# The written order of the opening dealt anew: linear attention followed by four expert layers on one core

## The chip, the cores and the metric

The kernel runs on one core of one Trainium2 chip. A core has five queues that each run their own list of instructions in order: PE (matmuls, with its weight loads PEld), ACT, DVE, POOL and SP. SP only issues DMAs; ACT and POOL issue some too. The metric is the device time of one launch in microseconds. Three runs of the kernel before gave 486.61 us as the median (486.33 to 486.74).

## What is computed

```python
def phi(x):                      # elu + 1
    return np.where(x > 0, x, np.exp(x) - 1.0) + 1.0
q_p, k_p = phi(q), phi(k)        # q, k, v: (8, 8, 576, 64), float32
kv = np.einsum('bhsd,bhse->bhde', k_p, v)
z  = np.sum(k_p, axis=2)
attn = einsum(q_p, kv) / (einsum(q_p, z)[..., None] + 1e-06)
x = attn.transpose(0, 2, 1, 3).reshape(4608, 512)
p = domain_probs / (domain_probs.sum(-1, keepdims=True) + 1e-09)
for e in range(4):               # w1: (4, 512, 1024), w2: (4, 1024, 512)
    out += p[:, e:e+1] * (np.maximum(x @ w1[e], 0) @ w2[e])
```

## The kernel before

**Tiles.** A batch has 576 rows: 512 make a tile, and the last 64 of each of the eight batches make a ninth tile. Tile j needs the attention of batch j, so the attention of batch j+1 is computed between the expert products of tile j. Each tile then passes four experts (two layers each); an expert is worked on as a unit (j, e) in two halves d.

**Layer 1** of a unit is a product of 2x2 blocks made with seven products instead of eight: steps p1, p2, p6, p7, p5, p4, p3 and the add c22 (class Block, L890 to L926). They need sums of weight blocks, made once by DVE: s{e}.0 to s{e}.3 (`weight_sums`, L745 to L751) for the first weights and t{e}.0 to t{e}.3 (L762 to L768) for the second, and sums of x blocks, ts{j}.0 to .3 (`token_sum`, L849). PE's products stand in L868 (`products`), ACT's copies in L879 and L894, the relu's in L901 and L922, and DVE's add with relu in L852. In the opening, tile 0 with expert 0 has a plain layer 1: steps L{g}{hf} (`layer1_half`, L655 and L664).

**Layer 2** of tile 0 is plain: y{e}.{ns}{part} (`layer2_part`, L715). From tile 1 on it is again made of seven products, m{j}{e}.{p}{i} (L810), that need sums of hidden blocks on POOL, hs{j}{e}.{d}{i} (L777 to L783). Results are weighted and added into `acc`, by ACT for the first (L704) and by DVE for the rest (L706), and stored by SP (L687). A step of several parts is written once for each part: for m10.51 the first mention emits its matmuls, the second its eviction.

**The opening.** Attention of batch 0 has its own code (class First): loads lq0-3, lk0-3, lv0-3 (L540, L548), exp on ACT (ke, qe: L563, L581), the linear part and the minimum on DVE or POOL (kl, ql, km, qm: L566, L584, L570, L587), the cast of v (vc: L573), transposes of q (qT: L595, copied in L597), kv products (kv: L606, copied in L617), numerators and denominators (nd: L628, divided in L631 and L632) and transposes of x (xT: L642, copied in L644). warm0 to warm4 are 14, 3, 2, 1 and 5 matmuls on zeros whose result nobody reads (L997).

**Loads of weights and of batch 1** are issued by POOL: w{layer}{e}{r} is a chunk of the first or second weights of expert e (L224, L227, L230); k0-3, v0-3, q0-3 are parts of batch 1 (L319); rk, rv its last 64 rows (L297). At most eight DMAs of POOL, and eight of SP and ACT together, are in flight: an issue waits for the landing of the one eight before. Later batches are loaded by SP: b1.load0 to 5 are the first six of batch 2's twelve loads, b2.load0 to 5 the other six, b1.loadlq the last 64 rows of batch 1's q, b1.next those of batch 2. The raw parts of all batches share six buffers (`praw`).

**The order** is explicit: each engine runs its instructions as they were emitted. CFG["EARLY"] (L87 to L119) is one list of step names; `advance` runs the next part of each named step, and each part puts its instructions at the end of the lists of the queues that it uses. EARLY covers the opening, tile 0 and half of tile 1; after it the steps left follow by numbers (the loop at the end). A queue runs its list strictly in order, so an instruction that waits holds all that stand behind it on its queue.

Of the kernel before, what the change touches and what calls it, by code (L numbers as in the profile page):

```python
# [84 lines left out]
    "WARM": (14, 3, 2, 1, 5),  # L85
    "BANK": {'qT0': 'py', 'qT1': 'b', 'nd00': 'py', 'nd00+': 'b', 'kv2': 'py', 'xT00': 'b', 'kv3': 'b', 'nd10+': 'b', 'L00': 'b', 'L10': 'py', 'nd01': 'b', 'xT01': 'py', 'nd11+': 'b', 'L20': 'e', 'L30': 'e', 'L01': 'e', 'L11': 'py', 'L21': 'py', 'L31': 'b', 'b1.qT3': 'py', 'b1.nd30': 'py', 'b1.nd21': 'b', 'b1.q1': 'b', 'b1.qT1': 'py', 'b1.nd01': 'py', 'b1.xT2': 'b', 'b1.nd11': 'py', 'b1.xT0': 'b'},
    "EARLY": (  # L87
        "lq2 lq3 lq0 lk0 qe0 ql0 ql3 qm0 kl0 lk1 lpr0 ke0 km0 qe2 ql2 qm2 lv0 ke1 kl1 km1 warm0 qT0 lv1 lk2 qe3 qm3 warm1 qT2 qT0 vc0 w100 warm2 kv0 vc1 qT2",
        "warm3 kv1 lk3 kv0 kv0 kl2 kv1 kl3 w102 kv1 nd01 lv3 nd01 warm4 xT11 xT01 ke2 km2 qT3 w103 vc3 lv2 ke3 vc2 nd00 w101 km3 xT01 w110 xT11 w111 kv3 k3 kv2",
        "qT3 lq1 nd00 qe1 xT00 w200 kv3 rk1 ql1 kv3 kv2 w201 qm1 L01 kv2 nd11 xT10 L31 qT1 v0 nd11 rv0 xT00 xT10 L10 xT21 rk0 xT21 v1 xT31 L11 qT1 xT31 nd10",  # L90
        "L01 L01 rv1 L31 w120 nd10 ts0.2 L00 ts0.0 xT30 ts0.1 xT20 L31 s0.0 L20 xT20 L30 xT30 L10 L10 L00 L00 L30 ts0.3 L30 p1.011 s1.0 p1.010 L11 L20 p1.010",
        "p2.010 s1.1 L20 w121 p2.010 p1.011 L21 L21 L21 s1.2 p6.010 p5.010 w210 L11 s1.3 p6.011 y0.30 p2.011 p6.010 p7.010 w211 p7.010 s0.1 p6.011 c22.010 v2",
        "y0.31 y0.00 p4.010 p2.011 y0.32 y0.33 p5.011 b1.k3 k0 pr0 y0.33 t0.0 t0.1 b1.km3 p7.011 p7.011 c22.011 y0.01 y0.02 y0.03 p4.010 b1.lk y0.20 y0.03 k2",
        "p4.011 s0.2 p3.010 p4.011 p3.011 y0.21 y0.10 y0.22 p3.010 y0.11 b1.v0 q1 k1 p1.021 y0.23 p1.021 p3.011 p1.020 s2.0 y0.12 v3 p2.021 b1.lv p1.020 t0.3",
        "s2.1 p2.020 s2.3 s2.2 y0.23 b1.v1 q0 t0.2 p6.020 p6.020 y0.13 p6.021 y0.13 y1.20 p7.020 y1.21 p2.020 p5.020 p7.020 w130 p2.021 y1.22 y1.23 t1.0 y1.10",
        "w131 p5.021 b1.v2 q3 b1.lkm y1.11 p6.021 b1.k0 b1.k2 b1.k1 w220 t1.1 t1.2 p7.021 y1.12 p7.021 c22.020 p3.020 y1.23 b1.v3 b1.km0 p4.020 p4.020 y1.00",
        "y1.01 q2 w221 y1.13 p4.021 b1.km2 b1.km1 b1.kv c22.021 p3.021 y1.02 y1.03 p1.030 p4.021 b1.q1 y1.30 y1.13 b1.load1 p1.031 b1.q0 p3.020 y1.31 p3.021",
        "p1.030 b1.qm1 b1.qT1 y1.32 y1.03 b1.qm0 s3.0 p1.031 w231 b1.qT0 s3.1 p2.030 y1.33 p6.030 b1.kv b1.qT0 p6.031 p2.031 b1.nd00 b1.nd01 b1.q3 p6.030 s3.3",
        "y1.33 p7.030 b1.loadlq p2.030 p5.030 b1.qm3 b1.qT3 p6.031 p7.030 w230 b1.qT1 b1.nd01 p7.031 p4.030 b1.qT3 s3.2 c22.030 b1.nd10 b1.nd11 b1.nd00 p2.031",
        "p3.030 b1.nd11 b1.nd10 p7.031 y2.00 y2.01 b1.nd30 p5.031 p4.031 p4.030 b1.next b1.nd31 b1.nd30 y2.20 b1.load0 b1.xT0 b1.lq b1.lqm b1.nd31 b1.q2 b1.qm2",  # L100
        "y2.21 b1.xT3 y2.02 c22.031 p4.031 b2.load2 y2.03 s0.3 b1.xT3 b1.qT2 y2.22 y2.23 b2.load1 b1.xT1 b1.load4 b1.load3 b1.load2 b1.qT2 b1.nd20 p3.031",
        "b1.xT1 p3.030 b1.nd21 y2.03 b1.xT0 b1.nd20 b1.nd21 y2.23 y2.10 y2.11 ts1.0 p1.101 p1.101 b1.load5 t1.3 b2.load0 t2.0 b1.xT2 y2.12 y2.13 b1.xT2 b2.k1",
        "ts1.1 lpr y2.30 y2.31 p1.100 p1.100 y2.32 y2.33 p3.031 p2.101 y3.20 y2.13 b2.km1 p6.100 b2.lk p2.100 t3.0 b2.load4 p2.101 p6.101 p6.100 p2.100 b2.lv",
        "ts1.2 p7.100 ts1.3 p7.100 b2.k0 y3.21 p5.100 y2.33 y3.22 t2.1 p4.100 y3.23 p6.101 p5.101 p4.100 p7.101 y3.30 c22.100 p3.100 b2.ones b1.qTl b2.v3 y3.00",
        "y3.01 p7.101 p4.101 b2.k2 b2.lkm y3.23 b2.km0 b2.load3 c22.101 b2.v1 y3.31 p3.100 t2.3 y3.32 p4.101 hs10.00 p3.101 b2.load5 y3.02 p1.110 b2.km2 y3.33",
        "p3.101 y3.03 b2.k3 b2.v0 b2.km3 b2.v2 b2.kv p1.110 y3.33 b2.load10 m10.21 b2.load7 p1.111 y3.03 y3.10 hs10.01 b1.qTl b2.q0 y3.11 p6.110 hs10.10",
        "hs10.02 y3.33 pr1 y3.12 y3.03 p1.111 m10.21 b2.q3 b2.load11 b2.qm0 y3.13 m10.51 hs10.11 p2.110 p6.111 p6.110 b2.q2 p2.111 m10.51 b2.qm3 y3.13 p2.110",
        "p6.111 t2.2 p7.110 m10.11 p5.110 m10.20 p7.110 b2.qm2 m10.11 b2.q1 c22.110 hs10.03 hs10.12 p7.111 m10.61 b2.qm1 t3.1 m10.20 p4.110 p4.110 p3.110",
        "p3.110 m10.50 p1.120 t3.2 b1.nl p2.111 p5.111 b3.load1 hs10.13 m10.61 m10.31 m10.31 m10.50 m10.10 p7.111 p4.111 b2.kv hs11.00 m10.10 m10.71 p1.120",
        "c22.111 t3.3 p6.120 m10.71 b2.lq b2.lqm p4.111 m10.60 b1.nl hs11.01 p3.111 p1.121 p6.120 y3.13 b2.load6 b2.qT m10.41 b2.qTl m10.60 m10.30 p2.120",  # L110
        "b2.nd1 p3.111 m10.41 m10.30 p7.120 b2.nd1 b2.nd0 hs11.10 y3.23 m10.70 m10.70 m11.21 hs11.11 p2.120 p5.120 m11.21 m10.40 p7.120 p4.120 hs11.03 p1.121",
        "p6.121 m11.20 m11.51 c22.120 p3.120 m10.40 b2.nd0 m11.20 p4.120 b3.k1 m11.50 m11.51 b3.km1 m11.11 p6.121 p2.121 m11.50 b2.nd1 b2.nd2 p3.120 p7.121",
        "m11.11 b2.nd3 b2.nd2 p1.130 hs11.02 p7.121 hs12.00 p2.121 b3.load0 b2.nd3 hs11.13 m11.10 m11.10 b2.next m11.61 m11.61 p5.121 p1.130 c22.121 p2.130",
        "m11.60 m11.31 p3.121 p6.130 m11.31 p4.121 b2.nd3 p6.130 hs11.12 m11.71 p4.121 p3.121 hs12.01 hs12.02 p2.130 m11.60 b2.nd4 hs12.10 p7.130 m11.71",
        "hs12.12 b2.nd5 p7.130 b2.nd2 b2.load8 m11.30 p5.130 p1.131 p1.131 m11.41 ts2.0 b2.nd4 b2.nd5 b2.nd5 m11.30 m11.41 m11.70 hs12.03 p6.131 p6.131 m12.20",
        "m11.70 m11.40 hs12.11 b3.ones c22.130 p4.130 p3.130 b1.xl p7.131 m12.21 p4.130 p7.131 m12.20 m11.40 b2.nl p2.131 b3.v0 p1.200 m12.21 b2.nl m12.50",
        "p2.131 m12.50 m12.51 p4.131 hs12.13 m12.51 ts2.1 p3.130 m12.10 m12.10 m12.11 m12.11 p5.131 p1.200 ts2.3 m12.60 m12.61 ts2.2 m12.60 b3.k0 m12.61",
        "c22.131 hs13.00 b2.load9 p4.131 p6.200",
    ),  # L119
}  # L120

# [1029 lines left out]
```

## Time and profile before

| | |
|---|---|
| median of three runs | 486.61 us |
| profiled execution: span from the first to the last instruction | 484.6 us |
| what lies around the span, by the median | 2.0 us |
| PE busy | 474.4 us (98%) |
| DVE, POOL, ACT busy | 377.3, 358.3, 332.2 us |
| bytes read from HBM, written | 45.16 MB, 9.44 MB |

The profile gives no separate time for the profiled execution, so its span stands beside the median. The page shows the busy share of each engine in 40 equal slices of 12.1 us. Times in the text are counted from the start of the span. The chain of waits follows the work that ended last back to its releasers; the waits say who held whom.

By stage (us busy of each 10 us stretch): from 0 to 10 PE is busy 6.82 us, from 10 to 20 8.32, and from 20 on nearly always. The DMA engines have a busy share of 0.80 in the first stretch and of 1.02 to 1.22 (more than one transfer overlaps on an engine) until 70 us.

### The profile page before, as it was taken

How to read it: one execution, taken by the hardware profiler on the slowest of the kernel's cores; microseconds unless marked ns; L12 is line 12 of the kernel's file. 1: busy time of each engine (PE TensorE's matmuls, PEld its weight loads, DVE VectorE, ACT ScalarE, POOL GpSimd, SP SyncE). 2: the span in 40 equal slices, each digit the busy share in tenths (PEclk: the TensorE clock that was granted, in tenths of full speed). 3: DMA queues.
4: the chain of work that ended last, by engine and by line, in shares of the span. 5: the costliest groups of instructions: out<-in, count | busy, mean ns of one | idle time of the engine just before them, and what ended most of it. 6: DMA issues, size and time to landing. Idle time of an engine off the chain costs nothing.

```text
span 484.6 us, 12013 instructions
## 1 busy us (share of the span) xinstructions
PE 474.4 (98%) x4565; PEld 407.2 (84%) x4565; DVE 377.3 (78%) x794; ACT 332.2 (69%) x662; POOL 358.3 (74%) x343
## 2 busy tenths in 40 slices
PE   6999999999999999999999999999999999999996
PEld 2766766898889888998889888988898888888885
DVE  5768987987868895888679886988687756775676
ACT  5689989956895599649884888478944565446530
POOL 5566044689966986789777977697769877987775
PEclk9999999999999999999999999999999999999999
DMA  8999987543445154523552446323221020002003
GB/s 293 216 217 254 233 204 201 134 109 88 123 144 111 42 156 150 120 53 115 172 135 56 114 133 157 77 77 106 69 59 28 7 93 2 1 0 89 2 1 87
DMA packets 79945, 53.67 MB, mean 111 GB/s; under 512 B 45152, under 2 KB 72608, under 8 KB 79888
## 3 DMA queue, kind: packets, MB, share of 16 engines
q1 hardware_dynamic: 69760, 40.43, 30.4%
q0 software_dynamic: 8896, 11.47, 12.3%
q10 hardware_dynamic: 1232, 1.02, 0.6%
q8 instruction: 35, 0.57, 0.5%
q14 instruction: 22, 0.18, 0.1%
HBM read 45.16 MB, written 9.44 MB: 113 GB/s over the span
## 4 chain that ended last, share of the span: by engine, by line
PE 90%; DMA 5%; DVE 2%; ACT 2%; issue 0%; POOL 0%; SPq 0%; ACTq 0%; DVEq 0%
PE py L810 38%; PE pb L868 24%; PE pe L868 18%; PE py L715 4%; DMA w<-in_moe_w_dram 2%; PE ph L655 1%; PE psum_nd L472 1%; DMA rawq<-in_q_dram 1%; DMA rawb<-in_q_dram 1%; DMA out_dram<-acc 1%; PE psum_kv L444 1%; PE pb L810 1%; PE pe L810 1%; DVE acc L706 0%; PE psum_nl L490 0%
## 5 line engine op out<-in xcount | busy, mean ns | idle before, releaser
L706 DVE SCALAR_TENSOR_TENSOR acc<-py,p_sb,acc 128x256 f32<-128x256 f32 (+1 forms) x382 | 182.2, 488 | 42.7 <-PE py L810 39.1
L852 DVE CUSTOM_DVE_ANT_0 h<-pe,u 128x512 f16<-128x512 f32 x140 | 96.1, 688 | 45.3 <-PE pe L868 28.0
L868 PEld LDWEIGHTS <-w 128*128 128x128 f16 x1120 | 108.9, 98 | 16.2
L777 POOL TENSOR_TENSOR hs<-h 128x512 f16<-128x512 f16 x64 | 74.7, 1167 | 56.9 <-DVE h L852 51.0
L810 PEld LDWEIGHTS <-h 128*128 128x128 f16 x1024 | 99.6, 98 | 12.2 <-issue 0.9
L810 PE MATMUL py<-w,h 128*128 128x256 f16 x744 | 106.4, 273 | 0.5 <-ACT acc L704 0.5
L879 ACT COPY u<-pb 128x512 f32<-128x512 f32 x140 | 82.4, 591 | 29.7 <-PE pb L868 27.8
L779 POOL TENSOR_TENSOR hs<-hs,h 128x512 f16<-128x512 f16 x64 | 74.1, 1157 | 26.8 <-PE py L810 24.3
L868 PEld LDWEIGHTS <-s 128*128 128x128 f16 x840 | 81.2, 98 | 12.6 <-DVE s L747 0.7
L868 PE MATMUL pb<-tt,w 128*128 128x256 f16 x560 | 83.8, 273 | 0.0
L810 PEld LDWEIGHTS <-hs 128*128 128x128 f16 x768 | 74.4, 98 | 8.8 <-issue 0.2
L783 POOL TENSOR_TENSOR hs<-h,hs 128x512 f16<-128x512 f16 x64 | 74.2, 1159 | 0.8 <-POOL h L781 0.5
L781 POOL TENSOR_TENSOR h<-h 128x512 f16<-128x512 f16 x64 | 74.6, 1165 | 0.1
L810 PE MATMUL py<-t,hs 128*128 128x256 f16 x496 | 74.1, 273 | 0.0
L901 ACT ACTIVATE h<-pe 128x512 f16<-128x512 f32 x70 | 41.9, 599 | 41.1 <-PE pe L868 40.5
L894 ACT COPY pe<-pb 128x512 f32<-128x512 f32 x70 | 40.0, 571 | 41.3 <-PE pb L868 15.8
L922 ACT ACTIVATE h<-pb 128x512 f16<-128x512 f32 x70 | 41.8, 599 | 6.3 <-PE pb L868 6.2
L868 PE MATMUL pb<-tt,s 128*128 128x256 f16 x280 | 41.9, 273 | 0.2 <-DVE s L747 0.2
L868 PE MATMUL pe<-tt,s 128*128 128x256 f16 x280 | 42.0, 273 | 0.0
L868 PE MATMUL pe<-xT,s 128*128 128x256 f16 x248 | 37.1, 273 | 0.0
L868 PE MATMUL pb<-xT,w 128*128 128x256 f16 x248 | 37.1, 273 | 0.0
L868 PE MATMUL pe<-xT,w 128*128 128x256 f16 x248 | 37.0, 273 | 0.0
(133 smaller groups left out, 594.6 us busy)
## 6 DMA issues: line engine op xcount, KB each, us to landing
out_dram<-acc SPq DMA_DIRECT2D x32, 256.0 KB, 2.5
w<-in_moe_w_dram POOLq DMA_DIRECT2D x14, 512.0 KB, 10.6
rawb<-in_k_dram SPq DMA_DIRECT2D x24, 256.0 KB, 3.1
rawb<-in_q_dram SPq DMA_DIRECT2D x24, 256.0 KB, 2.7
rawb<-in_v_dram SPq DMA_DIRECT2D x24, 256.0 KB, 2.8
w<-in_moe_w_dram POOLq DMA_DIRECT2D x4, 256.0 KB, 5.8
rawb<-in_k_dram POOLq DMA_DIRECT2D x4, 256.0 KB, 10.5
rl<-in_q_dram SPq DMA_DIRECT2D x16, 64.0 KB, 3.1
```

What stands on the lines that cost most here:

```text
L706: nc.vector.scalar_tensor_tensor(out=acc, in0=ps, scalar=pscal, in1=acc, op0=AO.mult, op1=AO.add)
L777: nc.gpsimd.tensor_tensor(out=hs[0], in0=a21, in1=a22, op=AO.add)
L779: nc.gpsimd.tensor_tensor(out=hs[1], in0=hs[0], in1=a11, op=AO.subtract)
L781: nc.gpsimd.tensor_tensor(out=a21, in0=a11, in1=a21, op=AO.subtract)
L783: nc.gpsimd.tensor_tensor(out=hs[3], in0=a12, in1=hs[1], op=AO.subtract)
L810: nc.tensor.matmul(out=ps, lhsT=lhsT(k), rhs=rhs[:, k], start=first and k == 0, stop=k == FH - 1, skip_group_check=True,)
L852: nc.vector._custom_dve(TENSOR_ADD_SAT, out=out, in0=ps, in1=u, s0=BIG, s1=0.0)
L868: nc.tensor.matmul(out=ps[:, kk], lhsT=lk(kc), rhs=rhs[:, kc], start=first and kk == 0 and kc == 0, stop=kc == 1, skip_group_check=True,)
L879: nc.scalar.copy(u, self.b)
L894: nc.scalar.copy(self.e5, self.b)
L901: nc.scalar.activation(self.h[:, :, 0, 0:NH], self.e5, AF.Relu)
L922: nc.scalar.activation(self.h[:, :, 1, 0:NH], self.b, AF.Relu)
```

## The change

Only the list EARLY is written anew. The same step names occur as often as before; instructions and buffers are the same, and so is everything after the list. The first lines, before:

```diff
-lq2 lq3 lq0 lk0 qe0 ql0 ql3 qm0 kl0 lk1 lpr0 ke0 km0 qe2 ql2 qm2 lv0 ke1 kl1 km1 warm0 qT0 lv1 lk2 qe3 qm3 warm1 qT2 qT0 vc0 w100 warm2 kv0 vc1 qT2
-warm3 kv1 lk3 kv0 kv0 kl2 kv1 kl3 w102 kv1 nd01 lv3 nd01 warm4 xT11 xT01 ke2 km2 qT3 w103 vc3 lv2 ke3 vc2 nd00 w101 km3 xT01 w110 xT11 w111 kv3 k3 kv2
-qT3 lq1 nd00 qe1 xT00 w200 kv3 rk1 ql1 kv3 kv2 w201 qm1 L01 kv2 nd11 xT10 L31 qT1 v0 nd11 rv0 xT00 xT10 L10 xT21 rk0 xT21 v1 xT31 L11 qT1 xT31 nd10
...
+lq2 ql2 rk0 rv0 lv1 warm3 rv1 warm4 warm1 lk0 lk1 lq0 lk3 lv0 w100 vc0 w102 w103 lk2 lv2 lq3 vc1 lq1 ke0 qe2 qm2 kl0 ql0 km0 warm2 warm0 qT2 qe0 ke1
+ql3 qm0 kl1 km1 lv3 lpr0 ke3 qT2 qe3 ke2 qT0 kv0 kv1 kv0 kv0 kv1 vc2 kl3 qm3 kl2 km2 b1.load5 kv1 km3 b2.load5 b1.loadlq qT0 w101 vc3 nd01 qe1 qT3
+nd01 kv2 nd00 kv2 nd00 ql1 xT11 kv3 w110 kv2 qT3 w111 xT01 qm1 xT11 kv3 kv3 xT01 xT10 xT00 nd11 L01 qT1 L11 nd11 xT00 xT10 qT1 xT21 xT31 xT21 L10 L31
...
+p2.010 ts0.0 ts0.1 ts0.3 s1.0 s1.1 w200 w201 k0 k3 rk1 w120 ts0.2 s1.3 pr0 w121 p6.010 p6.011 L10 p2.010 p6.010 p6.011 L21 p5.010 p7.010 y0.30 y0.00
...
+b1.k3 y0.10 p3.010 b1.km3 p3.011 s2.0 s2.1 w210 q0 k1 k2 w211 v0 v2 v1 q1 v3 w130
...
```

(the last `+` line is cut at both ends). What this does on the queues:

- **SP**: lq2, lv1, lk1, lq0, lk3, lv0, lk2, lv2, lq1, lv3, lpr0, then b1.load5, b2.load5, b1.loadlq. Before: lq2, lq0, lk1, lpr0, lv0, lv1, lk2, lk3, lv3, lv2, lq1, then b1.load1 and b1.loadlq, with b1.load5 and b2.load5 after b1.next.
- **POOL**: ql2, rk0, rv0, rv1, w100, vc0, w102, w103, w101, vc3, w110, w111, w200, w201, k0, k3, rk1, w120, w121, w210, q0, k1, k2, w211, the four v's with q1 among them, w130. Before: ql2, vc0, w100, w102, w103, vc3, w101, w110, w111, one k, w200, rk1, w201, v1, rv0, rk0, v0, rv1, w120, w121, w210, w211 and then the rest of batch 1.
- **ACT**: issues lk0 ahead of lq3; its exp's follow the new order of loads, and all four ke and three qe stand ahead of the first kvz copy.
- **PE**: the 25 matmuls of warm0 to warm4 all stand ahead of the first transpose; before, 14 stood there and 11 in between up to the first xT.
- **DVE**: s0.3 and s0.1 follow t0.0 and t0.1; s1.2 stands behind them (before it was made together with s1.0 and s1.1).

## The prediction

> **What bounds the kernel now.** I read the page first, then the table by stage, the chain, the waits of PE, the timeline of the first 45 us, and the DMA issues in narrow windows (an issue's start plus its time to landing is when its data is there).
>
> ```profile
> PE 474.4 (98%) x4565; PEld 407.2 (84%) x4565; DVE 377.3 (78%) x794; ACT 332.2 (69%) x662; POOL 358.3 (74%) x343
> ...
> PE   6999999999999999999999999999999999999996
> ...
> PEclk9999999999999999999999999999999999999999
> DMA  8999987543445154523552446323221020002003
> ```
>
> PE is busy in all slices but the first and the last, at full clock; the DMA engines are full in the first six slices (73 us). So only two things can move the end: how soon PE becomes saturated, and holes in its work afterwards. Over the first 130 us the trace has holes before 17 us (about 5.5 us in all, between short transposes and products), and then two:
>
> ```profile
> 42.60 9.66 DMA w<-in_moe_w_dram
> 52.36 0.70 DVE s L745
> 53.08 0.70 DVE s L747
> 53.83 1.05 PE pb L868 x8
> ...
> 85.93 0.47 ACT acc L704
> 86.45 0.60 PE py L810 x4
> ```
>
> In these lines of the chain (start, us, what) the last chunk of expert 3's first weights lands, DVE makes two weight sums of it, and PE starts 0.39 us after its last issue was through; at 86.45 us PE waited 0.5 us for an ACT eviction. What comes near to a third hole:
>
> ```profile
> 23.68 0.69 DVE L745 TENSOR_TENSOR s<-w 128x1024 f16<-128x1024 f16 x1 [1.21 <-DMA w<-in_moe_w_dram]
> ...
> 24.41 0.69 DVE L747 TENSOR_TENSOR s<-s,w 128x1024 f16<-128x1024 f16 x1
> ...
> 26.09 0.60 PE L868 MATMUL pb<-tt,s 128*128 128x256 f16 x4
> ```
>
> DVE starts s1.0 (first sum of expert 1's weights) the moment the weights land; the second sum is ready at 25.1 and PE uses it at 26.09. Only 1.0 us of slack. And from 11.3 to 23.9 us the weights' queue is always full:
>
> ```profile
> q0 software_dynamic: 2007, 2.66, 114.9%
> q1 hardware_dynamic: 166, 0.08, 2.1%
> ```
>
> q0 is what POOL issues, q1 what SP issues. Whatever else is put into the DMA engines before 24 us delays the weights byte for byte.
>
> **How I compare.** PE's list holds the same instructions in another order. I added up the work ahead of each row with the trace's durations (0.109 us for a 128x256 matmul, 0.216 for 128x512, 0.055 for a transpose, 0.0215 for a 64x65, 0.041 for each half of a numerator/denominator pair). Warm-up matmuls apart, from row 300 to row 1000 both lists have the same work ahead of the same row within 0.3 us. So "needed at" below is the time at which PE of the kernel before had done as much.
>
> **Part 1, the loads.** In SP's list the loads b1.load5 and b2.load5 (256 KB each, for batch 2) and b1.loadlq (2 x 64 KB) now follow the opening's loads directly; before, SP issued batch 1's leftover q at 45.0 us, the batch 2 loads from 63 on. Their buffers are free, so nothing holds them: each waits for a slot of the eight in flight, and I get issues from 8 to 10 us. On POOL rk0, rv0, rv1 (3 x 64 KB) now stand ahead of the first weight chunk. That is 832 KB ahead of the weights. Price: at the 406 GB/s of the 8-to-10 us stretch 2.1 us; by the 64 KB pieces (six landings from 65.1 to 66.0, 0.2 to 0.25 each) and 0.7 for each 256 KB, 2.4 to 2.7; if small pieces cost more beside weights, 3.0. I take 2.5, nearest to the measured pieces.
>
> Against it stands the slack of each chunk. Landing before: w101 at 11.85 + 6.0 = 17.85, w110 at 12.54 + 8.5 = 21.0, w111 at 13.25 + 10.3 = 23.6.
> - w101: needed at 20.2 (row 364): 17.85 + 2.5 = 20.35, late 0.2.
> - w110: needed at 22.6 (row 412): 23.5, late 0.9.
> - w111 through s1.0 and s1.1: needed at 26.5 (row 484), ready at 25.1 + 2.5 = 27.6, **late 1.1** (0.7 to 1.6 by the ends of the price).
> - w200, w201 follow w111 directly now (k0 and rk1 went behind them, 0.9 us back): late by under 1.1, hidden.
> - w210, w211: POOL puts q0, k1, k2 ahead of w211, some 3.3 us later, 44.7 against 44.1 needed: late 0.6, hidden by the lag that is there.
>
> **Part 2, the opening itself.** All 25 warm-up matmuls now stand ahead of the first transpose: 8 at the slow pace of the first 3.4 us (0.43 each) and 17 at 0.213 end near 8.3 us, where before PE met its first transpose at 7.37. qT2's copy then waits in ACT's list behind qe0, ke1, ke3 and the kvz copies behind ke2, about 11.3 instead of 10.38. On the other side the fillers between (11 matmuls, 2.3 us) are gone from the chain, and the two x_norm's stand closer. lv3, the last load, shares the engines with the weights and lands near 14 (10.8 before); POOL casts it (0.83), kv3 follows at 14.9. I get the first layer-1 product near 16.3 against 16.8 for the same work: a lead of 0.5 (0 to 0.8). It is worth nothing, because w110 and w111 are late next.
>
> **Part 3, the hole at 53.83.** Ahead of w131 stand b2.load5 and loadlq more than before, 384 KB or 1.0 us; s3.1 is ready near 54.9 where PE needs it at 54.17. A PE that runs 1.1 late loses no more there: the 0.39 of idle time is given back, and the lag is 0.75. Just before it, nd follows qT1's copy closely: ACT's nine pieces from the end of b1.kv sum to 4.6 us, PE's work to 4.34; up to 0.3, I take 0.1. w221 (59.2 by 2.6 per chunk) is needed at 58.3: lag 0.95 after it.
>
> **Part 4, the hole at 86.45.** PE waited since m10.11 stood behind m10.51's eviction. Now m10.11's matmuls come ahead of it: 0.5 back. Late next: two evictions in ACT's list need an `acc` buffer whose store must land, and SP issues those stores behind b3's load, which waits for ACT. In the trace the stores took from 80.27 to 85.4; shifted by 1 to 1.5 us they hold ACT to 87 or 88, and with it u2 and h, which PE needs at 87.8 to 90. I take 0.3 (0 to 0.7).
>
> **Sum.** 1.1 - 0.39 + 0.04 (s3.1's own limit) + 0.1 + 0.1 (w221) - 0.5 + 0.3 = 0.75 us; I add 0.25 for waits that I have not found, since a list of some 1,000 rows was dealt anew and before's has two: **+1.0 us**. The profiled execution spans 484.6 us; the median of the runs is 486.61, 2.0 more that lies around the span and stays. So 485.6 for the span, 487.6 for the time.
>
> **Rivals.**
> - *The loads are on time, and the refunds remain.* If the added bytes cost 2.1 us or less, or are served behind the weights, the lag is under 0.4, the lead of 0.5 holds, and 0.39 and 0.5 come back: 485.2. For: SP's loads and POOL's are separate queues. Against: in the stretch from 48 to 54 us they are served side by side. It decides where w111 lands before 25.0. Chance 0.15.
> - *All hidden.* Lag and refunds cancel: 486.4. Chance 0.10.
> - *The clock.* Before, fillers keep PE going in the gaps from 7.6 to 13.9; now gaps of up to 1.2 us between 8.3 and 16.3 stay empty, PE filled to a bit over half. The first 3.4 us of the trace show matmuls at half pace. If the pace falls back around 16 us for 3.4 us, 1.7 us of work come late, of which the weights would have cost 1.1: 488.2. Against: no gap is near 3.4 us. Chance 0.10. The Trainium skill ("TensorE: Matmul & The Clock Gate", Part 1: The HAM clock gate) says that the array falls to half clock after an idle window of about 3.4 us; by that rule this case stays away, and the trace before shows no fall between 5 and 480 us to test it on.
> - *ACT and the transpose.* The stores, or qT's transpose for batch 2 (4.4 us to landing, with 0.5 us of slack left instead of 1.9), hold PE for over a microsecond at 88 to 96: 488.8. Chance 0.10.
> - Forecast 0.55, itself 486.9 to 488.6; 0.40 of it above +0.2%.
>
> 0.2% (0.97 us) is what a measurement of this kernel can tell from no change. Slower: 0.40 + 0.09 (the clock) + 0.10 = 0.59. Faster: 0.13 of the first rival. Same: 0.15 of the forecast, 0.10 of all hidden, and 0.02 and 0.01 left of the first rival and the clock, 0.28. The range takes in the first rival and the last with its price doubled: 485.5 to 489.8.
>
> **What would show it.** In the changed kernel's profile: DVE's s<-w (L745) for expert 1 starts at 26 to 26.5 and is released by the weights; PE has idle time there, released by DMA w or DVE s, of about 1 us, and none at 86.45; the loads of batch 2 issue at 8 to 10 us. The forecast is wrong if w111 lands by 25.0, if PE's clock falls below full, or if a hole of over 0.5 us appears after 55 us other than those named.

## The result, and the profile after

The changed kernel takes 494.76 us (median of the runs, 494.14 to 495.12) where the kernel before took 486.65 us in the same runs: 8.1 us more, a ratio of 1.0164 with a 95% interval of 1.0149 to 1.0178. The forecast was 487.6 us. The profiled execution spans 492.8 us, 8.2 more than before. From the page of the kernel after (busy time of the engines; PE's busy tenths, its granted clock and the DMA share in 40 slices):

```profile
PE 478.2 (97%) x4565; PEld 408.8 (83%) x4565; DVE 377.7 (77%) x794; ACT 332.2 (67%) x662; POOL 357.2 (72%) x343
...
PE   8999999889999999999999999999999999999996
...
PEclk9899999999999999999999999999999999999999
DMA  8999976305455334633463244523231020002003
```

In PE's row an eight stands in slice 1 where a six stood (the warm-up matmuls), and two eights stand where nines stood (slices 8 and 9, 86 to 111 us); in the clock's row there is one (slice 2). Each engine runs as many instructions as before.

**Where the 8.2 us arise.** For every matmul I took the time from its start to the next one's start, less the usual step of that shape (0.109 us for 128x256), and added these up from the start of the span. This is the time that PE has lost, worked out from the trace. Its absolute size hangs on the usual steps that are taken for the small shapes; the differences between two runs hardly do:

```
us into the span       30     75     88     96    103    132    end
kernel before        9.05  10.25  11.65  11.71  11.72  11.76  16.20
kernel after        10.01  11.54  13.38  15.23  17.55  19.53  24.36
difference           0.96   1.29   1.74   3.52   5.83   7.77   8.16
```

Of 8.2 us, 1.3 arise before 75 us (opening and tile 0), 6.5 between 75 and 132 us (tile 1), 0.4 after that. PE's waits between 75 and 130 us (sum, times, longest) say for whom, first before, then after:

```profile
PE py L810 <- ACT acc L704: 0.5, 1, 0.5
```

```profile
PE py L810 <- DVE acc L706: 3.6, 4, 1.4
PE pe L868 <- ACT h L901: 1.7, 1, 1.7
PE pb L868 <- ACT pe L894: 0.2, 1, 0.2
```

L706 is an eviction: DVE adds a finished product of the second layer to `acc`, and only then is its `py` buffer free for the next product. The profile counts the idle time alone; with the drain of the product ahead (its last matmul runs on for 0.16 us past the point at which the next could have started), each such wait costs 0.16 us more from start to start. The chain of the kernel after (start, us, what) shows four of them:

```profile
78.88 1.06 DVE p_sum L264
79.96 0.36 DVE p_sum L265
...
81.80 0.75 DVE acc L706
82.54 0.04 issue
82.58 0.60 PE py L810 x4
...
93.61 0.47 ACT acc L704
94.08 0.47 ACT u L879
94.56 0.51 ACT h L901
95.06 0.04 issue
95.11 0.60 PE pe L868 x4
...
99.34 0.80 DVE acc L706 x2
100.13 0.04 issue
100.17 0.60 PE py L810 x4
...
101.91 0.50 DVE acc L706
102.41 0.04 issue
102.45 1.03 PE py L810 x8
```

At 82.58 (1.25 us lost) PE needs a buffer that y3.03 fills; its eviction stands on DVE behind pr1, 2.7 us of arithmetic on the probabilities. At 95.11 (1.84) PE's next product, p5.111, writes the buffer `pe`, which ACT's relu h has to read first; ACT's copy u and relu h stand behind the evictions m10.50 and m10.61, and ACT waited 1.95 us for the first of them. At 100.17 (1.58) m10.41 waits for the eviction m10.31, whose product had been done 3.5 us before. At 102.45 (0.74) m10.40 stands directly behind m10.30, which fills the other half of the same buffer.

DVE is not too full there. Busy time between 80 and 126 us (PE, PEld, DVE, ACT, POOL), before and after:

```profile
80.00:126.00 46.00, 45.52 (x454) 39.99 (x449) 38.85 (x85) 34.25 (x74) 37.40 (x34) 1.00 0.48 128
```

```profile
80.00:126.00 46.00, 40.26 (x393) 33.82 (x392) 33.56 (x71) 27.55 (x56) 30.92 (x28) 1.00 0.38 101
```

Every engine does less in these 46 us than before. They wait for each other.

**The opening.** The weights' queue is not alone any more between 11.3 and 23.9 us (queue, packets, MB, share), and DVE's first sum of expert 1's weights (s1.0) starts 2.2 us later than at 23.68 before:

```profile
q0 software_dynamic: 1598, 2.05, 89.9%
q1 hardware_dynamic: 1300, 0.76, 26.7%
```

```profile
19.58 0.69 DVE L745 TENSOR_TENSOR s<-w 128x1024 f16<-128x1024 f16 x1 [0.91 <-DMA w<-in_moe_w_dram]
...
25.84 0.69 DVE L745 TENSOR_TENSOR s<-w 128x1024 f16<-128x1024 f16 x1 [2.56 <-DMA w<-in_moe_w_dram]
26.57 0.69 DVE L747 TENSOR_TENSOR s<-s,w 128x1024 f16<-128x1024 f16 x1
```

The first of these lines is s0.0, a sum of expert 0's weights: it waits for w103, and DVE's copy of xT stands behind it, so that PE waits too (PE timeline):

```profile
20.52 1.39 PE L655 MATMUL ph<-xT,w 128*128 128x256 f16 x11 [0.32 <-DVE xT L644]
```

And the clock falls (stretch, its length, PE busy with matmuls, granted clock, DMA share, GB/s):

```profile
12.00:13.00 1.00, 0.01 (x2) 1.00 1.15 268
13.00:14.00 1.00, 0.98 (x18) 0.55 1.18 248
14.00:15.00 1.00, 1.00 (x27) 0.50 1.14 263
15.00:16.00 1.00, 1.00 (x24) 0.50 1.24 214
16.00:17.00 1.00, 1.00 (x16) 0.74 1.21 200
```

### The profile page after: what moved, and what is told of

Its sections match the earlier page's. It is cut to its first block, busy times and chain, and to the rows that moved or that the text cites. A ratio compares the mean times of both kernels' runs of the same rounds, so it can differ in the third digit from the quotient of the medians.

```text
span 492.8 us, 12018 instructions
## 1 busy us (share of the span) xinstructions
PE 478.2 (97%) x4565; PEld 408.8 (83%) x4565; DVE 377.7 (77%) x794; ACT 332.2 (67%) x662; POOL 357.2 (72%) x343
## 3 DMA queue, kind: packets, MB, share of 16 engines
q10 hardware_dynamic: 1232, 1.02, 0.7%
## 4 chain that ended last, share of the span: by engine, by line
PE 88%; DMA 3%; DVE 3%; ACT 2%; SPq 1%; issue 1%; POOL 1%; DVEq 0%; POOLq 0%
PE py L810 38%; PE pb L868 24%; PE pe L868 18%; PE py L715 3%; DMA w<-in_moe_w_dram 2%; DVE acc L706 2%; PE psum_nd L472 1%; DMA vraws<-in_v_dram 1%; PE ph L655 1%; PE psum_kv L444 1%; PE pb L810 1%; DVE h L852 1%; PE pe L810 1%; DMA praw<-in_moe_domain_probs_dram 0%; ACT pe L894 0%
## 5 line engine op out<-in xcount | busy, mean ns | idle before, releaser
L706 DVE SCALAR_TENSOR_TENSOR acc<-py,p_sb,acc 128x256 f32<-128x256 f32 (+1 forms) x382 | 182.0, 488 | 47.0 <-PE py L810 41.0
L779 POOL TENSOR_TENSOR hs<-hs,h 128x512 f16<-128x512 f16 x64 | 74.3, 1162 | 25.6 <-PE py L810 23.2
L704 ACT ACTIVATE acc<-py,p_sb 128x256 f32<-128x256 f32 (+1 forms) x68 | 32.5, 493 | 8.1 <-PE py L810 6.8
```

The source lines that it names most:

```text
L706: nc.vector.scalar_tensor_tensor(out=acc, in0=ps, scalar=pscal, in1=acc, op0=AO.mult, op1=AO.add)
L779: nc.gpsimd.tensor_tensor(out=hs[1], in0=hs[0], in1=a11, op=AO.subtract)
```

## The experiments

Ratios are to the kernel before, run beside each set on the same chip; "lost" is PE's lost time as above. First theory: the loss sits in tile 1, in the places of evictions on ACT and DVE. Rival: the late weights and the clock set off all the rest.

**1 and 2. Which half of the list.**

```diff
 steps 1 to 369 of the new list (up to the first product of tile 1)
-steps 370 to 713 of the new list
+the 344 steps left, in the order of the old list
```

> The first 369 steps of the new list (up to the first product of tile 1, some 75 us), the other 344 in the order of the old list. Time that PE lost, added up in both traces from the gaps between its matmuls: at 75 us the changed kernel has lost 1.3 us more than the kernel before, at 132 us 7.8 us more, and after that no more than 0.4 is added. Theory (the loss sits in tile 1, in the order of the evictions of the second layer on ACT and DVE): 486.65 + 1.3 = 487.9, between 487.2 and 489.2. Rival (the opening's late weights and the clock set off everything that is late afterwards): 492 to 495.

Measured: 1.0044 (1.0029 to 1.0059), 2.0 us lost more at 132 us, 2.2 at the end. PE's first new wait is for weights, w102's (PE timeline):

```profile
19.24 0.61 PE L655 MATMUL ph<-xT,w 128*128 128x256 f16 x4 [0.42 <-DMA w<-in_moe_w_dram]
20.93 1.39 PE L655 MATMUL ph<-xT,w 128*128 128x256 f16 x11 [0.19 <-DVE xT L644]
```

The second is the mirror image, 378 old steps and the rest in the new order.

> The mirror image: the first 378 steps of the old list (up to the first product of tile 1), the rest in the order of the new list. Theory (tile 1's order): 486.65 + 6.5 = 493.2, between 491.5 and 494.5. Rival (the opening carries it): 486.5 to 488.5.

Measured: 1.0191 (1.0173 to 1.0208), 495.9 us on the scale of the expectation and above its range. So the part up to tile 1 costs 2.1 us and the rest of the list 6 behind the new head, or 9.3 behind the old one. The two don't add: behind the old head PE waits 0.78 and 1.43 us at 72.9 and 75.7 for u and h, and 2.0 at 84.2. The rival is out: with the new head and the old order behind it most of the loss is gone, and with the old head ahead of the new order all of it is there.

**3. Five fillers moved into the gap.**

```diff
-... warm3 warm4 warm1 ... nd01 qe1 ...
+... warm3 warm1 ... nd01 warm4 qe1 ...
```

> The new list with one step moved: warm4 (five of the 25 warm-up matmuls) stands behind the first numerators and denominators, in the gap from 11.84 to 13.02 us, as in the old list. Theory (the clock fell because PE had little to do from 9.1 to 13.0 us): the granted clock stays at 1.0 from 13 to 16.5 us, where the changed kernel has 0.5 to 0.74; PE has lost about 1.3 us less at 17 us. Of that up to 0.9 reaches the end, since w111 lands at 25.6 and its sums then bind: 493.9 to 494.7. Rival (the fall has nothing to do with the fillers): the clock is 0.5 again and the time 494.7 to 495.2.

Measured: 1.0166 (1.0149 to 1.0183). The expectation missed: with 20 matmuls at the start, PE was idle for 1.75 us ahead of 9.83, and the clock fell earlier and for longer, from 11.24 to 18.07 us. PE had lost 2.6 us more than the kernel before at 30 us, and the end shows no difference to the changed kernel that the runs can tell.

**4. Two of the waits mended**, without a PE instruction moved.

```diff
-... pr1 c22.101 ... y3.03 y3.33 b2.kv ...
+... c22.101 ... y3.03 y3.33 pr1 b2.kv ...
-... m10.50 m10.61 p7.111 p2.111 p5.111 ...
+... p7.111 p2.111 m10.50 m10.61 p5.111 ...
```

> The new list with three steps moved, no PE instruction among them: pr1 (2.7 us of DVE work on the domain probabilities) behind the evictions y3.03 and y3.33, for which PE waited 1.25 us at 82.6; the evictions m10.50 and m10.61 on ACT behind the copy u and the relu h of p7.111 and p2.111, for which PE waited 1.84 us at 95.1. Theory (each such wait is made by the place of an eviction in the list of ACT or DVE): 494.76 - 3.1 = 491.7 if nothing else is late next, 493.2 if half of it comes back. Rival (PE would have to wait there anyway for something else, weights, stores or DVE's total load): 494.3 to 495.2.

Measured: 1.0108 (1.009 to 1.0126), lost at the end 21.99 instead of 24.36: 2.4 of 3.1 us came back. Both waits are gone, and a new one stands at 89.08 (PE timeline, its waits of 80 to 104 us):

```profile
89.08 0.60 PE L810 MATMUL py<-t,hs 128*128 128x256 f16 x4 [0.69 <-DVE acc L706]
93.71 0.60 PE L810 MATMUL py<-w,hs 128*128 128x256 f16 x4 [0.17 <-ACT acc L704]
98.34 0.60 PE L810 MATMUL py<-t,h 128*128 128x256 f16 x4 [1.41 <-DVE acc L706]
100.62 0.60 PE L810 MATMUL py<-t,h 128*128 128x256 f16 x4 [0.57 <-DVE acc L706]
```

**5 and 6. Clock and loads**, each on the base of the first.

```diff
-"WARM": (14, 3, 2, 1, 5)
+"WARM": (19, 3, 2, 1, 5)
-... warm3 warm4 warm1 ... nd01 qe1 ...
+... warm3 warm1 ... nd01 warm4 qe1 ...
```

> As the first experiment (new list up to tile 1, old order behind), with warm4 moved behind the first numerators and denominators and warm0 made 19 instead of 14, so that 25 warm-up matmuls still stand ahead of the first transpose and five more fill the gap at 11.8 us. Theory (the clock falls when PE has been mostly idle over some 3.4 us, wherever the idle time lies): granted clock 1.0 throughout from 13 to 17 us, and PE has lost 7.6 to 8.2 us at 17 us where the first experiment has 9.1. The gain is mostly given back to the first weights, which land at 17.4 to 20.6: 10.0 lost at 30 us, a ratio of 1.003 to 1.0045 to the kernel before. Rival (something else holds the clock low): 0.5 again from 13 us.

Measured: 1.008 (1.0055 to 1.0104), a miss. The clock fell at 11.66, before the five fillers came, and they ran at half pace for 2.3 us in the way of what follows.

```diff
-... kl2 km2 b1.load5 kv1 km3 b2.load5 b1.loadlq qT0 ...
+... kl2 km2 kv1 km3 qT0 ...
-lq2 ql2 rk0 rv0 lv1 warm3 rv1 ...
+lq2 ql2 lv1 warm3 ...
-... k0 k3 rk1 w120 ...
+... k0 k3 rk1 rk0 rv0 rv1 w120 ...
...
+(b1.loadlq behind w220; b1.load5 and b2.load5 in the old order behind tile 1's first product)
```

> As the first experiment, with the loads that the change pulled forward put back: b1.load5 and b2.load5 in the old order behind the first product of tile 1, b1.loadlq behind w220, rk0, rv0 and rv1 behind rk1. Theory (832 KB ahead of the weights delay them by about 2 us): w103 lands near 17.3 instead of 19.3, w111 near 23.6 instead of 25.6, PE's waits at 19.2 us (0.58, for the weights) and at 20.9 (0.35) shrink, and at 30 us PE has lost 9.3 to 9.8 instead of 10.28: ratio 1.0025 to 1.0035. Rival (the loads of SP cost the weights nothing): landings and ratio as in the first experiment, 1.0044.

Measured: 1.0005 (0.9996 to 1.0015), better than expected. w111 lands at 23.2 instead of 26.1 in the first experiment, w102 at 15.0 instead of 19.2; the two waits are gone, and at 30 us PE has lost 8.53 where the first has 10.28 and the kernel before 9.05. So with the loads back the new head costs nothing that the runs can tell. Part of the 1.9 us between the two experiments may come by way of the clock: of the first experiment's runs, five with a mean granted clock of 0.991 to 0.993 took 489.5 to 490.1 us, and two with 0.994 and 0.995 took 488.6 and 488.5; eight of the sixth's twelve have 0.996 or more. The two parts are not separated. In the four runs of the changed kernel the time does not follow the clock (494.14 us at 0.991, 494.58 at 0.995).

**7 and 8. Evictions.** In the old list every eviction of m10 to m12 stands ahead of the next product on its `py` buffer; in the new one ten of 42 stand behind it. From end of product to start of eviction the kernel before takes 0.12 us in the median, and 3 of 42 take over 1 us; the kernel after 0.55, and 16 of 42, up to 7.4.

```diff
-... m10.50 m10.10 p2.111 ... t3.3 m10.50 m10.61 ...
+... m10.50 m10.50 m10.10 p2.111 ... t3.3 m10.61 ...
...
(nine more in the same way)
```

> The whole new list, with ten evictions of the second layer moved (m10.51, m10.31, m10.50, m11.50, m11.60, m11.30, m11.51, m11.71, m12.51, m12.50): in the new list each stands behind the next product on the same py buffer, in the old list none of the 42 does; here each stands directly ahead of that product. Nothing of the opening, of PE's order or of pr1 is changed. Theory (an eviction listed behind the next product on its buffer has to wait for that product too, though it writes the other half, and holds what stands behind it on ACT or DVE): the waits of PE at 95.1 (1.84) and 100.2 us (1.58) go or shrink to under 0.8 each, PE has lost 2 to 4 us less at 132 us: 490.8 to 492.8. Rival (evictions are late because ACT and DVE have too much other work ahead of them, and the place against the next product makes no difference): 494 to 495.2.

Measured: 1.018 (1.0166 to 1.0193). The theory in this form falls. The waits went from ACT and DVE to PE (its timeline, four of nine):

```profile
92.70 0.60 PE L810 MATMUL py<-w,h 128*128 128x256 f16 x4 [0.56 <-ACT acc L704]
98.13 0.60 PE L810 MATMUL py<-w,h 128*128 128x256 f16 x4 [0.68 <-DVE acc L706]
101.79 0.60 PE L810 MATMUL py<-t,h 128*128 128x256 f16 x4 [0.57 <-DVE acc L706]
108.74 0.60 PE L810 MATMUL py<-w,h 128*128 128x256 f16 x4 [1.65 <-DVE acc L706]
```

The eighth does the same, with pr1 behind y3.03 and y3.33 as in the fourth and further evictions moved up (shown against the changed kernel):

```diff
-... m10.31 m10.60 b1.nl t2.3 ... m10.71 b2.lqm p3.111 m10.70 m10.31 ...
+... m10.31 m10.31 b1.nl t2.3 ... m10.71 m10.70 b2.lqm p3.111 ...
...
```

> As the seventh, and besides pr1 behind the evictions y3.03 and y3.33, and twelve further evictions of tile 1 moved up in the list of their engine to where the trace of the changed kernel shows their product done. Theory (tile 1 loses its time at evictions that stand too late, and nothing else is short there): PE has lost at most 2 us more in tile 1 (75 to 132 us) than the kernel before, which loses 1.5 there: 488.9 to 490.5. Rival (DVE and ACT are too full between 80 and 126 us; evictions brought forward only hold up the adds h and copies u): 491.5 to 494.

Measured: 1.022 (1.0205 to 1.0236), the slowest, and above what either side expected. Evictions moved up on DVE and ACT hold up the relu h for which PE waits (1.5 us at 96.6), and PE still waits at 88.9 (1.9) and 110.3 (2.6).

Second theory, from these lines: it is the distance on PE. Added up from PE's lists, at least 0.87 us of PE's work (two steps of four matmuls) stand between two products on one `py` buffer in the old list; in the new one six of 36 stand at 0 to 0.44. A product directly behind another has to wait 0.74 us, for the drain and the eviction, though it writes the other half of the buffer.

**9 and 10. Distance.** The ninth moves seven products back on PE on the base of the seventh, for example:

```diff
-... m10.30 m10.40 m11.20 hs11.10 ... p7.120 p2.120 ... p5.120 p1.121 ...
+... m10.30 m11.20 hs11.10 ... p7.120 p2.120 ... p5.120 m10.40 p1.121 ...
...
```

> The whole new list as in the seventh experiment (each eviction of tile 1's second layer ahead of the next product on its py buffer), and besides m10.11, m10.10, m10.60, m10.40, m11.11, m11.70 and m12.10 moved back on PE until at least 0.87 us of PE's work (two steps of four matmuls) stand between two products on one py buffer. In the old list the least distance is 0.87 us; in the new list six of 36 stand at 0 to 0.44. pr1 stays where the new list has it. Theory (a product has to wait until the last one on its buffer is evicted, 0.74 us after a product right behind it; where the list puts two together, moving the eviction only changes who waits): the waits for evictions that the seventh experiment has from 88 to 124 us (8 of them, 6.7 us) go to under 2.5 us in sum; lost at 132 us 15 to 17, where the seventh has 20.7; ratio to the kernel before 1.004 to 1.010. Rival (DVE and ACT have too much to do in this stretch): ratio 1.014 or more.

Measured: 1.0136 (1.0121 to 1.015), 2.1 us better than the seventh, and between what the two theories expected. Its waits for evictions from 88 to 124 us are down from 6.7 us to 2.8 (1.02 at 97.6, 1.73 at 108.3); waits for h of 0.4 to 0.7 each came up.

The tenth does the one thing in the kernel before:

```diff
-... m10.70 ... (0.87 us of PE's work) ... m10.40 ...
+... m10.70 m10.70 m10.40 ...
...
```

> The kernel before with one thing of the change alone: six products (m10.40, m10.71, m11.11, m11.40, m12.10, m12.11) moved up on PE directly behind the product ahead of them on the same py buffer, whose eviction is moved up between the two. Nothing else is touched, neither loads nor opening. Theory (distance on the buffer): each of the six makes PE wait about 0.74 us, 4.4 in all, of which little can be hidden since PE is saturated there: ratio 1.006 to 1.010. Rival (products at distance 0 cost nothing by themselves, only evictions that are late for other reasons do): 0.999 to 1.002.

Measured: 1.0127 (1.0109 to 1.0145), more than expected: at 132 us PE has lost 6.2 us more than in the kernel before. PE's waits between 90 and 124 us, where the kernel before has none:

```profile
92.84 1.03 PE L810 MATMUL py<-w,h 128*128 128x256 f16 x8 [0.66 <-DVE acc L706]
99.37 0.60 PE L810 MATMUL py<-t,h 128*128 128x256 f16 x4 [0.58 <-DVE acc L706]
103.16 0.60 PE L810 MATMUL py<-w,h 128*128 128x256 f16 x4 [0.58 <-DVE acc L706]
104.85 0.60 PE L810 MATMUL py<-t,hs 128*128 128x256 f16 x4 [0.49 <-DVE acc L706]
115.11 0.60 PE L810 MATMUL py<-t,h 128*128 128x256 f16 x4 [0.58 <-DVE acc L706]
120.55 0.60 PE L810 MATMUL py<-w,h 128*128 128x256 f16 x4 [0.58 <-DVE acc L706]
122.16 0.60 PE L810 MATMUL py<-w,h 128*128 128x256 f16 x4 [0.58 <-DVE acc L706]
```

Six products moved, with their evictions, in a list of 713 steps cost three quarters of what the whole change costs. Each of the six pairs has its wait: five are alike, 0.58 us idle and 0.16 of drain, and the one at 92.84 has 0.66; the one at 104.85 follows from the pair ahead of it. With the drain the seven come to 5.2 of the 6.2 us. In two of the pairs (m10.70 to m10.40, m11.70 to m11.40) the second product goes on in the half that the first one filled, in the other four it writes the other half, and they wait alike. The Trainium skill ("PSUM — Partial Sum Buffer", PSUM bank collisions raise a hardware error) says that accesses of two engines have to be kept apart by bank, or by bank and quarter of the partitions, and not by address. The trace of the changed kernel agrees: a `py` buffer is 128x512 float32, 2 KB in each partition, and m10.40 writes the half that m10.30's eviction does not read, and yet waits for it (0.58 us idle at 102.45). No run here leaves such a wait out.

**11. Loads back and the clock held.**

```diff
-"WARM": (14, 3, 2, 1, 5)
+"WARM": (25, 2, 3, 2, 1)
-... qT2 qe0 ... qT0 kv0 kv1 kv0 ... nd01 qe1 ...
+... qT2 warm4 qe0 ... qT0 warm1 kv0 kv1 warm2 kv0 ... nd01 warm3 qe1 ...
```

> The sixth experiment (new opening, loads put back, old order from tile 1) with 25 warm-up matmuls at the start and eight more in four gaps: one behind the first transposes, two behind the second, three behind the first kv products, two behind the first numerators. In the traces so far the granted clock changes on a grid of 3.41 us; stretches of that grid in which the matmuls' own time came to 0.30 to 0.50 were followed by half clock, those with 0.51 and more were not. Theory (the share of work in such a stretch decides): the eight fillers (1.7 us) bring it to 0.7 or more, the clock stays at 1.0, and PE has lost about 1 us less at 17 us than in the sixth (8.30); little of the weights is late there, so 0.5 to 1.2 us reach the end: ratio 0.998 to 1.0000. Rival (the clock falls anyway, or the fillers delay the transposes): 1.000 to 1.003.

Measured: 1.0005 (0.9994 to 1.0016), as the sixth, and not the 0.998 to 1.0000 expected. The clock stays up:

```profile
13.00:14.00 1.00, 1.00 (x26) 1.00 1.27 224
14.00:15.00 1.00, 1.00 (x30) 1.00 1.19 184
15.00:16.00 1.00, 0.73 (x13) 1.00 1.26 207
```

At 17 us PE has lost 6.68 us and spent 1.7 on added fillers, 8.4 in all, where the sixth has 8.30: half a clock for 3.4 us costs nothing here that the fillers don't cost. For a longer stretch this is not shown (see the sixth).

**12. The second layer's steps where the old list has them.**

```diff
-(m10 to m12 and hs10 to hs13 as in the new list)
+(the same steps as in the old list, counted by the first layer's steps ahead of them)
```

> The whole new list, but all steps of tile 1's second layer in it (products and evictions m10 to m12 and the hidden sums hs10 to hs13) stand where the old list has them, counted by the steps of the first layer ahead of them. Loads, opening, pr1, attention of batch 2 and first layer stay as in the new list. Theory (the dealing of these steps is what costs over 5 us): lost at 132 us 14.5 to 17 where the changed kernel has 19.5, ratio 1.005 to 1.010. Some pairs on one buffer are still at 0.44 to 0.66, and pr1's 1.25 us stay. Rival (the new places of the attention's divisions and of pr1 on DVE carry it): 1.014 or more.

Measured: 1.0201 (1.0185 to 1.0216), a miss: products then wait for hidden sums (1.7 us at 85.8) and evictions (1.6 at 107.5) that the rest of the new list makes late.

**13 and 14. Single places on DVE and ACT mended on top of the ninth**, and the loads put back on top of that.

```diff
-... m10.31 m10.60 b1.nl t2.3 p4.111 m10.31 ... m10.71 b2.lqm ...
+... m10.31 m10.60 m10.31 b1.nl p4.111 ... m10.71 t2.3 b2.lqm ...
-... t3.2 p6.121 ... b2.nd0 b3.km1 m11.51 m11.50 ... m11.51 m11.10 ...
+... p6.121 ... m11.50 b2.nd0 b3.km1 m11.51 ... m11.51 t3.2 m11.10 ...
...
(pr1 as in the fourth, b2.q1 behind p4.110)
```

> As the ninth experiment (products on one py buffer at least 0.87 us apart, each eviction ahead of the next product), and besides, on DVE: pr1 behind y3.03 and y3.33, the eviction m10.31 ahead of b1.nl's division and the weight sum t2.3 behind m10.71, the eviction m11.50 ahead of b2.nd0's division, the weight sum t3.2 behind m11.51; on ACT b2.q1 behind the relu of p4.110. PE's waits that this aims at, by the ninth's trace: 1.24 us at 82.9, 1.02 at 97.6, 1.73 at 108.2, 0.42 at 92.0, 4.4 in all. Theory (tile 1's loss is the sum of such single places in the lists, and can be taken away one by one): PE has lost 19 to 21 us at the end, where the ninth has 23.9 and the kernel before 16.2; ratio 1.004 to 1.009. Rival (the lists of ACT and DVE are coupled so tightly there that mending one place makes another late): 1.011 or more.

Measured: 1.0109 (1.0095 to 1.0122), at the edge of what the rival expected. Of 4.4 us of waits aimed at, 1.7 came back in the trace (22.16 lost instead of 23.85); the wait at 82.9 is gone, the others shrank or moved.

> As the thirteenth, with the loads that the change pulled forward put back as in the sixth (b1.load5, b2.load5, b1.loadlq, rk0, rv0, rv1). Theory (the two parts of the loss, loads in the opening and places in tile 1, add): 2 us less than the thirteenth; ratio 1.000 to 1.005. Rival (tile 1's waits take up what the opening gains, as they did with the opening's lag in the second experiment): as the thirteenth within 0.7 us.

Measured: 1.01 (1.0085 to 1.0115). At 75 us PE has lost 2.5 us less than in the thirteenth; a new wait of 1.14 at 85.6 takes part of it, 1.6 are left at the end of the trace, and 0.7 in the medians. The two parts of the loss do not simply add.

**15. The two holes of the kernel before.**

```diff
-... q0 t0.2 ... w130 ... w131 ...
+... t0.2 ... w130 ... w131 q0 ...
-... b2.q2 p2.111 m10.51 b2.qm3 ...
+... p2.111 m10.51 b2.q2 b2.qm3 ...
```

> The kernel before with the two waits taken away that the prediction named: q0's load behind w131's (so w131 lands 0.7 us sooner, and the hole of 0.39 us at 53.8 closes), and b2.q2's two ACT instructions (1.1 us) behind the eviction m10.51 (so that m10.11 does not wait 0.5 us at 86.45). Theory: 0.4 to 0.9 us less than the kernel before, ratio 0.998 to 0.9992. Rival (other work is late at once: q0's own data, the qp of batch 2): 0.9995 or more.

Measured: 1.0036 (1.0023 to 1.0049), slower. In place of 0.39 and 0.5 us, PE waits 0.35 at 53.1 for the transposes of batch 1's q0, whose minimum DVE makes later now, and 1.09 at 88.3 for a relu h that stands behind b2.q2 on ACT. None of the runs beats the kernel before.

## Why the prediction was wrong

- **Direction: right; size: wrong**, 1.0 us forecast, 8.1 measured, and the range (to 489.8) missed.
- **Part 1, the loads: the delay and its size were right, the path was not.** w111 landed at 25.8 (23.6 before, forecast 26.1), and PE's lag at 30 us was 0.96 (forecast 1.1). It arose one stage earlier than said, at chunks that I had not priced: w103, landing at 19.48 instead of 16.53, holds s0.0 and with it the copy of xT for which PE waits at 20.5 us, and in the first experiment w102 makes PE wait at 19.2; s1.1 was ready (27.2) when PE came to it (27.3). That the lag came so near to the forecast is therefore partly luck. By the first and the sixth, the loads cost 1.9 us (1.0044 against 1.0005), since they also eat the lead of part 2, and in part perhaps by way of the clock.
- **Part 2, the opening: right once the loads are away** (a lead of 0.5 at 30 us in the sixth). In the changed kernel the first layer-1 product comes at 16.87, forecast 16.3.
- **The clock rival came true in its event** (half clock from 13.1 to 16.5) **and not in its price**: 1.7 us of late work was forecast; the sixth and eleventh show none for a stretch of 3.4 us. "No gap is near 3.4 us" was the wrong test (below).
- **Part 3:** the refund of 0.39 at 53.83 was 0.1: 0.32 of PE time is lost there still, now to ACT's copy of qT. Up to 75 us the sum says 0.95, measured 1.29.
- **Part 4 and the sum: this step failed.** The hole at 86.45 did go (0.7 back, forecast 0.5). But "I take 0.3 (0 to 0.7)" for what is late next and "0.25 for waits that I have not found" stand against 6.5 us net in tile 1. I had compared the two lists by the work ahead of each row of PE, and found them alike within 0.3 us up to row 1000. That comparison is blind to two things that both lists show without a run: how far two products on one buffer stand apart on PE, and whether an eviction stands ahead of the next product on its buffer and of which other work on ACT and DVE. And it ended at row 1000, near 58 us; the list goes on to row 2100, near 126 us, twice the rows that the sum spoke of. What I had named as late next, the stores (and qT's transpose, the last rival), did not come: between 75 and 130 us no wait of PE, ACT or DVE that the profile of the changed kernel lists ends at a DMA.
- The fifteenth shows besides that a hole counted as a refund is not free: what is moved out of its way arrives late elsewhere.

**What stays open.** Shown are the 1.9 us of the loads (with what the clock adds to them), about 2.4 us of two misplaced groups (fourth), the price of a closed pair (tenth; three stand among the changed kernel's main waits, at 102.5, 114.2 and, by ACT, ahead of 95.1), and that neither DVE's load nor any one wait carries the rest. How the 6 us divide among the places can't be settled: mending them one after the other gave 2.7 us in all (1.0164 to 1.0109), each time with a new wait close by, and no version with the new order of tile 1 came near 1.0044.

## What to carry to other kernels

When an order of steps is dealt anew, compare for every buffer the distance between two writers on the saturated engine, and for every release its place in its own queue; equal work ahead of equal rows proves nothing. Where PE is saturated, a release has to fit into the distance (here 0.74 us into 0.87), so one step moved can cost the whole of it. An allowance for waits not found should be sized by the length of the list that was not compared, and a hole in a tuned order counted as a refund only if what fills it is early elsewhere.

## What the runs showed of the hardware

The granted clock changes on a grid of 3.41 us. In 11 of the 17 traces it fell in the opening, for 3.41 or 6.83 us. What goes with it is not an idle gap but the share of a stretch of the grid that the matmuls' own time fills (0.213 us for 512 columns, half of the 0.427 that the warm-up matmuls take at half clock, placed from their starts in the traces; good to about 0.05). The full-clock stretches ahead of a fall had 0.32 to 0.49 (0.40 in the changed kernel, 0.47 in the sixth experiment); those with 0.50 (the second) and more were followed by full clock. Two stretches do not fit, the first full-clock stretch of the tenth (0.45) and of the fifteenth (0.47), after which the clock stayed up, so the share is not the whole of the rule. The longest idle time of PE in the stretch ahead of the fall was 1.0 us in the changed kernel and 1.75 in the third experiment.

The grid's place against the span's start differs from run to run: the first full clock came at 4.1 to 7.2 us. Eight traces have the same opening; where the first full clock came at 6.3 us or later (the changed kernel, the first, fourth and eighth) the half clock lasted 3.41 us, where it came at 5.7 or earlier (the seventh, ninth, twelfth and thirteenth) 6.83. The rule of the Trainium skill ("TensorE: Matmul & The Clock Gate", Part 1: The HAM clock gate) that the prediction quotes, an idle window of 3.4 us, is too lenient for these traces.
